# Attention in chunks of 64 tokens instead of 128, with 64 by 64 products, a scan for the states and a new order of the engines

## The chip, the cores and the metric

The kernel runs on one core of a Trainium2 chip. A core has TensorE (matrix products, PE in the profile; its weight loads are listed as PEld), VectorE (DVE), ScalarE (ACT), GpSimd (POOL) and SyncE (SP, which issues the DMAs here). The metric is the device time of one execution in microseconds (us); the median of three executions counts.

## The reference, cut to what matters

Three stages follow each other on inputs of 2 batches, 768 tokens and 8 heads of 48 channels. The change lies in the first.

```python
def _attn_ref(r, k, v, w, u):              # each (2, 8, 768, 48); u is (8, 48)
    state = np.zeros((B, H, D, D))
    for t in range(S):
        kt, vt, rt, wt = k[:, :, t], v[:, :, t], r[:, :, t], w[:, :, t]
        cur = np.einsum('bhd,bhe->bhde', u[None] * kt, vt)
        y[:, :, t] = np.einsum('bhd,bhde->bhe', rt, state + cur)
        state = wt[:, :, :, None] * state + np.einsum('bhd,bhe->bhde', kt, vt)
```

The second stage, on the heads joined to 384 channels, is a gated layer: `h = gelu(x @ w_in)`, its half `v` is normalised, mixed over the tokens by `w_sg`, multiplied with the half `u`, sent through `w_out` and added to `x`. The third stage mixes each token with the one before it and computes `sigmoid(xr @ w_r) * (relu(xk @ w_k)**2 @ w_v)`.

## The kernel before, in words

The tokens of a batch are cut into two halves of 384 (`TB`); batch and half give the group g = 0 to 3. A unit of attention is one group and one pair of heads, so there are 16 units (`units`, 4 in each group). The two heads of a pair lie on partitions 0 to 47 and 64 to 111. The sequential recurrence is replaced by chunks of `C` = 128 tokens. Within a chunk the running products of the decays w are made by a scan of VectorE, r is multiplied and k is divided by them, and what remains are matrix products. The preparation is done for packs (12, three in each group; the fourth pair of a group is collected from spare partitions of the three packs by DMAs into the tile `six`).

The steps, with the letter that each has in the written order: for a pack, `L` and `q` load, `D` (L267) and `g` (L274) are the two scans of 387 elements, `j` (L271) takes reciprocals, `d` (L278) multiplies r and k in, `K` (L282) makes r times k, `f` is a check on ScalarE, `6` moves the spare rows. For a unit, `w` loads v; `T` (L327) transposes the keys on TensorE and `k` (L331) copies them out of PSUM on ScalarE; `A` (L338) are the scores of keys against queries, `P` (L345) the sums for the present token; `m` (L378) masks the scores and `n` (L384) weighs v, both on VectorE out of PSUM; `S` (L354) are the products keys times v of one chunk; `s` (L365) adds the state before to them by a product with the identity, and `x` (L373) multiplies with the chunk's decay on ScalarE, which gives the state after the chunk; `J` (L394), `N` (L398) and `I` (L404) add up the output in PSUM; `O` (L408, L411) copies it out on ScalarE and `o` shares the fourth pair's rows out by DMAs.

The other letters are dense stages on full 128 by 128 products: `v` and `u` are the two halves of `x @ w_in`, `M` the mixing over tokens, `W` the product with `w_out`, `E`, `R` and `Z` the products of the third stage. `C` converts weights (`x`, `b`, `t` and `o` are VectorE's parts of it, `h` is ScalarE's; C0 to C2 are the weights that `v` needs, C3 to C5 those of `u`), `X` splits x into a high and a low part, `e` is a product whose result nobody reads and which keeps TensorE busy. `v0.2` is the first dense product; it needs the splits X0.2 and the weights C0, C1 and C2. A generator token such as `v0.2` stands once for each of its steps.

All instructions are issued in the order of one string, `ORDER` (L37): a token emits its instructions, each engine executes its own in that order, and semaphores are placed by the framework from the tiles that are read and written. The fp32 products of the attention stand in the trace as two loads and two matmuls each; the dense ones are three products of rounded halves (`mm3`, L207 to L209).

PSUM has eight banks here: three for `ps_d` (dense products), two for the scores `pA` (`ps_A`), two buffers of one bank for the outputs `py` (`ps_y`), one for `ptr` and `pkv` (`ps_t`).

Of the kernel before, what the change touches and what calls it, by code (L numbers as in the profile page):

```python
# [36 lines left out]
ORDER = """L0 D0 j0 e e e e e e e g0 f0 e L1 D1 q0 d0 j1 e e e e e e e e K0 g1 Q q1 L2 w0 q2 w1 A0 P0 T0 e e e e e e f1 k0 S0.0 S0.1 x0.0 m0 d1 n0 K1 J0 s0.1  # L37
S0.2 A1 x0.1 s0.2 P1 x0.2 C1.l D2 j2 g2 m1 d2 C1.x n1 61 w2 L3 K2 C1.b C0.l 60 62 e T1 e e N0 k1 S1.0 S1.1 x1.0 J1 s1.1 S1.2 I0 A2 x1.1 s1.2 P2 C1.r
x1.2 f2 O0 e e T2 e D3 n2 m2 j3 C0.x C0.b C0.t C1.t g3 e N1 k2 S2.0 S2.1 x2.0 J2 s2.1 S2.2 I1 A3 C1.q O1 P3 x2.1 s2.2 x2.2 f3 w3 q3 L4 m3 K3 D4 n3 j4
d3 e e T3 N2 e e k3 S3.0 S3.1 C0.h x3.0 J3 s3.1 S3.2 N3 x3.1 I3 O3 A4 I2 s3.2 P4 x3.2 e T4 e e e k4 w4 q4 C2.l C2.r S4.0 s4.0 S4.1 L5 x4.0 g4 d4 K4 n4  # L40
m4 A5 s4.1 P5 J4 C5.l o3 w5 q5 o3 D5 C0.o C2.x m5 n5 j5 f4 O2 x4.1 C1.h 63 o3 T5 k5 N4 e e S5.0 s5.0 S5.1 J5 x5.0 C2.q s5.1 x5.1 X0.2.h X0.0.h N5 I4
I5 C2.b g5 d5 K5 C2.t T6 C2.h C5.r k6 w6 64 L6 w7 X0.2.l C1.o C2.o v0.2 S6.0 s6.0 S6.1 65 X0.0.l D6 C5.x j6 C5.b A7 C5.q X0.1.h x6.0 O4 C0.r s6.1 g6
O5 f6 x6.1 P7 C5.t C5.h v0.0 T7 n7 m7 v0.2 k7 A6 S7.0 P6 s7.0 S7.1 J7 X0.1.l q6 C3.l C3.x K6 C3.b n6 d6 C5.o C7.l C4.l C4.x w8 L7 q7 q8 m6 C3.t C4.b
C4.t C0.q x7.0 s7.1 C7.h C3.r x7.1 v0.1 N7 T8 I7 A8 v0.0 f5 k8 C3.h O7 C3.q C4.h v0.0 C3.o D7 P8 S8.0 S8.1 J6 N6 o7 j7 C4.o n8 g7 m8 d7 u0.0 u0.3 I6
A9 C4.r x8.0 v0.0 f7 s8.1 S8.2 C7.o K7 P9 m9 O6 v0.1 x8.1 J8 s8.2 v0.0 x8.2 u0.0 C8.l C9.l w10 o7 L8 C11.l L9 w9 o7 D8 K8 j8 g8 d8 n9 q9 B 68 66 N8
u0.1 T9 u0.2 v0.1 v0.2 k9 C9.h S9.0 S9.1 C8.h X1.0.h X1.2.h x9.0 u0.2 C11.h C11.o X1.0.l C9.o X1.2.l I8 A10 P10 s9.1 S9.2 x9.1 J9 s9.2 v0.2 x9.2
X1.1.h X1.1.l u0.1 v0.1 v1.0 N9 T10 C8.o 67 D9 j9 n10 m10 v0.0 C4.q f8 k10 u0.3 u1.1 S10.0 S10.1 I9 A11 x10.0 O8 P11 s10.1 S10.2 x10.1 v1.0 J10 q10
w11 C6.l C16.l L10 s10.2 u1.2 x10.2 C6.h v0.2 T11 v1.0 v1.1 C10.l K9 g9 d9 D10 j10 K10 n11 v0.2 C6.o g10 m11 O9 u1.2 v0.1 f9 v0.1 v1.0 k11 C10.h C10.o
v1.2 S11.0 S11.1 J11 v1.1 x11.0 s11.1 S11.2 x11.1 v1.2 d10 A12 s11.2 P12 C19.l w12 C14.l L11 x11.2 v1.1 u1.0 N10 T12 u1.1 C14.h C14.o m12 n12 N11 u1.3
I11 v1.2 k12 v1.1 C16.h C16.o v1.2 O11 u1.0 A13 I10 O10 S12.0 P13 s12.0 S12.1 J12 x12.0 v1.0 v1.0 s12.1 C15.l C15.h x12.1 v1.1 w13 C17.l o11 q11 v1.2  # L50
o11 69 o11 X2.0.h C19.r v1.1 v1.2 D11 j11 g11 d11 m13 n13 K11 C15.o N12 M0.1 T13 M0.2 M0.2 A14 I12 X2.2.h X2.1.h X2.1.l C19.x C19.b C19.t C17.h C17.o
k13 P14 S13.0 f11 s13.0 S13.1 J13 611 C13.l w14 w15 C12.l 610 C24.l m14 n14 M0.1 x13.0 s13.1 x13.1 O12 u1.3 f10 C19.q M0.0 N13 T14 I13 C13.h k14 A15
P15 m15 X2.0.l M0.2 M0.1 C13.o S14.0 s14.0 S14.1 J14 x14.0 s14.1 C24.r x14.1 C12.h O13 N14 v2.0 T15 n15 M0.0 X2.2.l C24.x C24.b C24.t M0.3 M0.3 C18.l
k15 S15.0 s15.0 S15.1 J15 x15.0 s15.1 x15.1 N15 I15 O15 C24.q C12.o I14 O14 C21.l | C19.h C24.h C21.r v2.2 v2.2 C21.q v2.0 C18.r C18.q C19.o C24.o
C21.x v2.1 M0.0 C18.x M0.3 C18.b C18.t C21.b C21.t M1.1 C26.l C20.l v2.2 C18.h C18.o M1.1 M1.2 C26.r v2.2 C26.x M1.1 M1.2 M1.3 M1.0 v2.1 G0.3.h C21.h
C21.o v2.1 v2.0 C20.x C26.b C20.b C20.t C26.t M1.3 M1.3 C26.h v2.1 v2.0 v2.0 v2.2 v2.1 u2.2 v2.0 C20.h G0.3.l M1.0 M1.0 v2.1 u2.0 G0.1.h G0.0.h G0.0.l
G0.1.l v2.2 C20.o u2.2 C26.q u2.1 u2.3 u2.0 u2.1 G0.2.h u2.3 C20.r o15 o15 o15 X3.2.h C20.q C34.l C27.l C27.r X3.1.h C25.l C27.q C25.r X3.0.h C25.q
C27.x G0.2.l W0.2 W0.0 C27.b C27.t X3.1.l C26.o W0.2 v3.1 W0.1 X3.0.l X3.2.l v3.1 C25.x W0.1 C25.b v3.1 v3.2 v3.0 C27.h C27.o C25.t v3.1 v3.1 C34.x
C34.b W0.0 v3.2 v3.0 v3.0 v3.2 u3.3 u3.2 u3.3 u3.0 u3.1 u3.2 v3.0 C34.r C25.h C25.o C34.t v3.0 C23.l C22.l C28.l v3.2 C34.q u3.1 v3.2 v3.1 v3.0 C22.r
G1.3.h G1.0.h G1.1.h v3.2 M2.3 M3.2 C22.x M1.2 C22.b C22.t C22.h u3.0 C22.q C34.h C22.o M3.2 M3.2 C34.o C28.x C28.b C28.t C28.h C28.o G1.0.l M2.1 M2.1  # L60
C28.r C28.q G1.2.h C35.l C35.x M2.2 M2.2 C23.x C37.l M3.3 C35.r C35.b C35.t G1.2.l C35.h C35.q C35.o G1.3.l C38.l C23.b C23.t C23.h C38.r M2.2 M2.3
G1.1.l M2.3 M2.0 C23.o M2.0 M2.0 M3.3 W1.0 W1.0 C37.x W1.2 W1.1 C38.x M2.1 G2.1.h G2.1.l C38.b G2.0.h G2.0.l W1.1 C37.b W1.2 C38.q C37.r C37.q G2.2.h
G2.2.l M3.0 M3.1 G2.3.h G2.3.l C37.t C23.r M3.0 H0 Y0.0.0.a C38.t Y0.0.2.a Y0.1.0.a M3.3 C31.l C29.l C36.l W2.2 M3.1 Y0.0.1.a C23.q Y0.1.0.b C31.r
Y0.0.0.b Y0.0.1.b Y0.0.0.c W2.2 Y0.0.1.c C37.h C37.o Y0.1.2.a C31.q Y0.0.2.b Y0.0.2.c M3.0 M3.1 C36.x W2.0 W2.1 W2.1 Y0.1.1.a C36.b C36.t E0.0 C36.r
Y0.1.2.b C36.q E0.0 C36.h Y0.1.1.b E0.0 Y0.1.0.c C36.o W2.0 E0.2 E0.0 C38.h E0.1 E0.5 Y0.1.1.c Y0.1.2.c C38.o E0.0 C31.x E0.1 F E0.2 C31.b C31.t C29.x
R0.0 R0.0 C29.r E0.1 E0.1 G3.0.h R0.2 E0.2 C29.b C29.t E0.1 C29.h C29.o C30.l C32.l C33.l E0.3 E0.4 G3.1.h E0.3 E0.2 C31.h E0.3 C31.o R0.2 E0.3 E0.3
E0.5 C32.x C30.x C30.b C30.t G3.3.h C30.h E0.5 G3.3.l C30.o E0.2 E0.7 R0.1 R0.1 E0.6 C29.q C33.x C33.b C33.t E0.4 E0.4 C32.b C32.t C32.h C33.h E0.4
C33.o E0.5 E0.5 C32.o E0.4 E0.6 E0.6 E0.7 E0.7 E0.7 E0.6 H1 E0.6 C33.r Y1.0.0.a Y1.0.0.b Y1.0.2.a E0.7 C33.q Y1.0.1.a Y1.1.1.a Y1.0.0.c Z0.0 Z0.1 Z0.2
Z0.3 Z0.4 Z0.5 Z0.6 Z0.7 Y1.0.1.b Y1.0.2.b Y1.0.1.c Y1.0.2.c E1.0 E1.0 E1.0 Y1.1.0.a Y1.1.0.b E1.0 E1.0 z0.1 E1.2 E1.2 E1.1 E1.5 z0.2 E1.2 E1.1 E1.1
E1.1 E1.2 Y1.1.2.a Y1.1.2.b Y1.1.2.c E1.2 E1.5 Y1.1.1.b G3.1.l E1.5 E1.5 E1.1 E1.6 E1.6 Y1.1.0.c z0.0 E1.5 E1.3 Z1.0 Z1.1 E1.4 E1.7 Z1.2 E1.3 E1.3  # L70
E1.3 G3.2.h G3.0.l E1.3 Z1.3 E1.6 Y1.1.1.c E1.6 E1.6 G3.2.l R1.0 W3.2 y0.1 y0.2 y0.0 H2 Y2.0.0.a Y2.0.1.a Y2.0.0.b Y2.0.1.b E1.4 E1.4 E1.4 Y2.0.1.c
Y2.0.2.a Y2.0.0.c Y2.0.2.b Y2.0.2.c E2.0 E2.0 Y2.1.1.a E1.4 R1.1 Z1.4 Z1.5 Z1.6 R1.0 R1.1 E1.7 E1.7 Y2.1.0.a W3.2 E1.7 E1.7 Z1.7 R1.2 W3.0 E2.1 E2.0
# [851 lines left out]
```

## Time and profile before

| | us |
|---|---|
| median of 3 runs | 332.86 (332.62 to 333.13) |
| the profiled execution | 332.0 |
| its span, first to last instruction | 330.2 |
| first dense product starts (in the span) | 36.66 |
| last product of the attention, next dense product starts | 116.76 |
| TensorE busy | 321.7 |
| VectorE busy | 232.7 |

Times in rows are microseconds from the span's start unless marked ns. A row of instructions gives the engine, the line of the code, the operation, what it writes and reads, the shape and how many there were (x12). Matmuls are pipelined and their listed durations overlap: what one costs is read from the distance between starts.

### The profile page before, as it was taken

How to read it: one execution, taken by the hardware profiler on the slowest of the kernel's cores; microseconds unless marked ns; L12 is line 12 of the kernel's file. 1: busy time of each engine (PE TensorE's matmuls, PEld its weight loads, DVE VectorE, ACT ScalarE, POOL GpSimd, SP SyncE). 2: the span in 40 equal slices, each digit the busy share in tenths (PEclk: the TensorE clock that was granted, in tenths of full speed). 3: DMA queues.
4: the chain of work that ended last, by engine and by line, in shares of the span. 5: the costliest groups of instructions: out<-in, count | busy, mean ns of one | idle time of the engine just before them, and what ended most of it. 6: DMA issues, size and time to landing. Idle time of an engine off the chain costs nothing.

```text
span 330.2 us, 6938 instructions
## 1 busy us (share of the span) xinstructions
PE 321.7 (97%) x2721; PEld 299.3 (91%) x2721; DVE 232.7 (70%) x427; ACT 180.9 (55%) x440; POOL 28.6 (9%) x78
## 2 busy tenths in 40 slices
...
GB/s 188 229 272 208 141 217 177 209 196 113 77 84 178 98 70 109 64 128 66 48 95 50 4 143 48 95 3 0 48 26 0 3 48 21 5 0 24 50 24 54
DMA packets 16501, 29.82 MB, mean 90 GB/s; under 512 B 2256, under 2 KB 12496, under 8 KB 16464
## 3 DMA queue, kind: packets, MB, share of 16 engines
...
q8 instruction: 22, 0.36, 0.4%
q14 instruction: 15, 0.12, 0.1%
...
## 4 chain that ended last, share of the span: by engine, by line
PE 91%; DVE 3%; DMA 2%; ACT 1%; POOL 1%; issue 1%; SPq 0%; ACTq 0%; DVEq 0%
PE po L565 12%; PE pk L207 5%; PE ps L207 5%; PE pk L208 5%; PE pk L209 5%; PE ps L209 5%; PE ps L208 5%; PE po L209 4%; PE po L208 4%; PE po L207 4%; PE pA L338 3%; PE pu L207 3%; PE py L394 3%; PE py L404 3%; PE pu L209 3%; PE pu L208 3%
## 5 line engine op out<-in xcount | busy, mean ns | idle before, releaser
L539 DVE TENSOR_TENSOR kr<-kr 128x384 f32<-128x384 f32 x32 | 17.4, 555 | 22.5 <-ACT kr L537 22.3
L207 PE MATMUL ps<-wsg,vn_hi 128*128 128x384 f32 x96 | 32.8, 341 | 0.0
L207 PE MATMUL pk<-xk_hi,wk_hi 128*128 128x384 f32 x96 | 32.6, 339 | 0.0
L209 PE MATMUL pk<-xk_hi,wk_lo 128*128 128x384 f32 x96 | 32.5, 338 | 0.0
L208 PE MATMUL pk<-xk_lo,wk_hi 128*128 128x384 f32 x96 | 32.5, 338 | 0.0
L209 PE MATMUL ps<-wsg,vn_lo 128*128 128x384 f32 x96 | 32.4, 338 | 0.0
L208 PE MATMUL ps<-wsg,vn_hi 128*128 128x384 f32 x96 | 32.4, 338 | 0.0
L537 ACT ACTIVATE kr<-pk 128x384 f32<-128x384 f32 x32 | 15.6, 491 | 24.9 <-PE pk L209 18.8
L544 ACT CAST kk_hi<-kr 128x384 fp32r<-128x384 f32 x32 | 16.0, 511 | 19.1 <-DVE kr L539 14.9
L546 DVE TENSOR_TENSOR kk_lo<-kr,kk_hi 128x384 fp32r<-128x384 f32 x32 | 17.7, 555 | 11.7 <-ACT kk_hi L544 11.2
L565 PE MATMUL po<-pl_win_hi,kk_hi 128*128 128x384 f32 x81 | 23.1, 339 | 0.0
L565 PE MATMUL po<-pl_win_lo,kk_hi 128*128 128x384 f32 x63 | 18.4, 339 | 0.0
L207 PEld LDWEIGHTS pk<-xk_hi,wk_hi 128*128 128x128 f32 x96 | 18.0, 188 | 0.3 <-DVE xT L504 0.3
L565 PE MATMUL po<-pl_win_hi,kk_lo 128*128 128x384 f32 x54 | 18.3, 339 | 0.0
L207 PE MATMUL pu<-xs_hi,win_hi 128*128 128x384 f32 x48 | 16.9, 352 | 1.4 <-ACT v L453 1.4
L207 PEld LDWEIGHTS ps<-wsg,vn_hi 128*128 128x128 f32 x96 | 18.0, 188 | 0.1
L208 PEld LDWEIGHTS ps<-wsg,vn_hi 128*128 128x128 f32 x96 | 18.0, 188 | 0.0
L208 PEld LDWEIGHTS pk<-xk_lo,wk_hi 128*128 128x128 f32 x96 | 18.0, 188 | 0.0
L209 PEld LDWEIGHTS ps<-wsg,vn_lo 128*128 128x128 f32 x96 | 18.0, 188 | 0.0
L209 PEld LDWEIGHTS pk<-xk_hi,wk_lo 128*128 128x128 f32 x96 | 18.0, 188 | 0.0
L378 DVE TENSOR_TENSOR am<-pA,c_sb 128x768 f32<-128x768 f32 x16 | 15.1, 946 | 3.3 <-PE pA L345 3.3
L208 PE MATMUL po<-ga_lo,wout_hi 128*128 128x384 f32 x48 | 16.2, 337 | 0.0
(208 smaller groups left out, 902.2 us busy)
## 6 DMA issues: line engine op xcount, KB each, us to landing
...
```

Source lines behind the costliest of these rows:

```text
L207: T.matmul(ps, lh, rh, start=(i == 0), stop=False)
L208: T.matmul(ps, lh, rl, start=False, stop=False)
L209: T.matmul(ps, ll, rh, start=False, stop=(i == n - 1))
L338: T.matmul(u.pA[q:q + 64, h, c * C:(c + 1) * C], u.kinv[o:o + D, c, q:q + 64], u.rp[o:o + D, c, :], start=True, stop=True)
L378: V.tensor_mul(u.am.rearrange("p h (c t) -> p h c t", c=NCB), u.pA[:, :, :TB].rearrange("p h (c t) -> p h c t", c=NCB), mask[:, None, None ...
L394: T.matmul(u.py[64 * h:64 * h + m, cs], u.vk[:, c, h * D:h * D + m], u.am[:, h, cs], start=(c == 0), stop=False)
L404: T.matmul(u.py[o:o + D, c * C:(c + 1) * C], u.state(c)[o:o + D, :], u.rp[o:o + D, c, :], start=False, stop=(c == NCB - 1))
L537: A.activation(kr, ps, AF.Relu)
L539: V.tensor_mul(kr, kr, kr)
L544: A.copy(hi, kr)
L546: V.tensor_sub(lo, kr, hi.bitcast(F32))
L565: T.matmul(pv[g][s], l, wv[i][r], start=st, stop=(i == KF - 1 and l is ll))
```

## The change: what it does

Chunks have 64 tokens (`CA`), six in a half (`NA`). Each product of the attention is cut so that its operands are at most 64 by 64, and the four pairs of (rows 0 or 64, columns 0 or 64) of the array are taken in turn (`QUAD`). This holds for `A`, `P`, `S`, `J` and `N`; `I` has its rows and columns on the same head, so it uses two of the four. `N` is now an ordinary product with the identity instead of a transposition. `s` is gone. `x` happens once in a unit instead of once in a chunk: ScalarE copies all six products of keys and v out of PSUM, for the second half VectorE adds the state that the first half left, and one scan of VectorE over 48 times 7 elements makes all states (each row of seven ends with a zero, which restarts it). The decays that it multiplies with are laid out by a second copy of ScalarE in `k`. The scans of a pack write a tile `sc` of which there is one, `d` writes the packed tile, `j` also copies the chunk decays on GpSimd. `pA` and `pkv` now share one pair of banks (`tag="ab"`, one buffer), and `py` is one buffer of two banks. The four multiplications that made `uu` on GpSimd are gone. The order of all engines is new; it has 44 `e` instead of 39.

```diff
+CA = 64
+NA = TB // CA
-WL = NCB * (C + 1)
-PK = 2 * WL + TB
+WL = NA * (CA + 1)
+PK = 3 * TB + NA
-    ps_y = ctx_a.enter_context(tc.tile_pool(name="ps_y", bufs=2, space=PSUM))
+    ps_y = ctx_a.enter_context(tc.tile_pool(name="ps_y", bufs=1, space=PSUM))
+    QUAD = ((0, 0), (1, 1), (0, 1), (1, 0))
         def decays(u):
+            u.sc = ap1.tile([P, 2 * WL + 2], F32, name=f"sc_{u.n}", tag="sc")
+            V.tensor_tensor_scan(u.sc[:, :WL], u.wt[:, :WL], d1pat, 0.0, ALU.mult, ALU.add)
         def divide(u):
+            u.pk = ap3.tile([P, PK], F32, name=f"pk_{u.n}", tag="pk")
+            d = d1w.rearrange("p (c j) -> p c j", c=NA)[:, :, CA:CA + 1]
+            V.reciprocal(d, chunks(u.sc, 0)[:, :, CA:CA + 1])
+            G.tensor_copy(u.pk[:, 3 * TB:], chunks(u.sc, 0)[:, :, CA:CA + 1].rearrange("p c o -> p (c o)"))
         def keys(u):
             A.copy(u.kT, u.ptr)
+            u.fd, u.kv = fds[u.i % 2], kvs[u.i % 2]
+            A.copy(u.fd[:, :, :NA], u.W[:, None, :].broadcast_to([R, D, NA]))
         def scores(u):
+            u.pA = ps_A.tile([P, 2, 512], F32, name=f"pA_{u.n}", tag="ab")
             for c in range(NCB):
-                for h, q in ((0, 0), (1, 64), (0, 64), (1, 0)):
-                    o = 64 * h
-                    T.matmul(u.pA[q:q + 64, h, c * C:(c + 1) * C], u.kinv[o:o + D, c, q:q + 64], u.rp[o:o + D, c, :], start=True, stop=True)
+                for h, q in QUAD:
+                    o, t, s0 = 64 * h, 64 * q, c * C + q * CA
+                    T.matmul(u.pA[t:t + 64, h, c * CA:(c + 1) * CA], u.kinv[o:o + D, s0:s0 + CA], u.rp[o:o + D, s0:s0 + CA], start=True, stop=True)
         def sums(u):
...
+                for h, q in QUAD:
+                    o, t = 64 * h, 64 * q
+                    k = u.home()[o:o + D, 2 * TB + c * C + t:2 * TB + c * C + t + CA]
+                    T.matmul(u.pA[t:t + 64, h, NCB * CA + c:NCB * CA + c + 1], k, c_sb[o:o + D, CU + u.p:CU + u.p + 1], start=True, stop=True)
         def states(u, c):
...
+                u.pkv = ps_A.tile([P, 2, 512], F32, name=f"pkv_{u.n}", tag="ab")
+                u.sx = ap2.tile([R, D, NA + 1], F32, name=f"sx_{u.n}", tag="sx")
+            for h, q in QUAD:
+                o, t, m = 64 * h, 64 * q, (64, D)[h]
+                T.matmul(u.pkv[o:o + m, q, c * D:(c + 1) * D], u.kT[t:t + 64, c, o:o + m], u.vk[t:t + 64, c, h * D:(h + 1) * D], start=True, stop=True)
-        def carry(u, c):
-            for h in range(2):
-                o, m = 64 * h, (64, D)[h]
-                T.matmul(u.pkv[o:o + m, c, :], ident[:, o:o + m], u.state(c), start=False, stop=True)
         def fade(u, c):
-            A.activation(o, u.pkv[:R, c, :], AF.Copy, scale=u.W[:, c, :])
+            A.copy(u.kv[:, :, :NA].rearrange("r e (c q) -> r e c q", q=2), u.pkv[:R, :, :NCB * D].rearrange("r q (c e) -> r e c q", c=NCB))
+            if u.hf:
+                V.tensor_add(u.kv[:, :, 0], u.kv[:, :, 0], Slast[u.p])
+            flat = "r e n -> r (e n)"
+            V.tensor_tensor_scan(u.sx.rearrange(flat), u.kv.rearrange(flat), u.fd.rearrange(flat), 0.0, ALU.add, ALU.mult)
+            if not u.hf:
+                Slast[u.p] = ap1.tile([R, D], F32, name=f"sl_{u.n}", tag=f"sl{u.p}")
+                G.tensor_copy(Slast[u.p], u.sx[:, :, NA - 1])
         def weigh(u):
-            u.am = ap2.tile([P, 2, TB], F32, name=f"am_{u.n}", tag="am")
+            u.am = ap2.tile([P, 2, NCB * CA], F32, name=f"am_{u.n}", tag="am")
...
         def inner(u):
...
+                for h, q in QUAD:
+                    o, t, m = 64 * h, 64 * q, (64, D)[h]
+                    T.matmul(u.py[o:o + m, q, c * CA:(c + 1) * CA], u.vk[t:t + 64, c, h * D:h * D + m], u.am[t:t + 64, h, c * CA:(c + 1) * CA], start=(c == 0), stop=False)
         def inject(u):
             for c in range(NCB):
-                T.matmul(u.py[:, c * C:(c + 1) * C], u.vg[:, c, :R], eye, start=False, stop=False, is_transpose=True)
+                for h, q in QUAD:
+                    o, t, m = 64 * h, 64 * q, (64, D)[h]
+                    T.matmul(u.py[o:o + m, q, c * CA:(c + 1) * CA], u.vg[t:t + 64, c, o:o + m], eye[t:t + 64, t:t + 64], start=False, stop=False)
         def outer(u):
...
+                for h, q in QUAD:
+                    n, o = 2 * c + q, 64 * h
+                    if u.state(n) is not None:
+                        T.matmul(u.py[o:o + D, q, c * CA:(c + 1) * CA], u.state(n)[o:o + D, :], u.rp[o:o + D, n * CA:(n + 1) * CA], start=False, stop=(c == NCB - 1))
```

Of the order, the stretch from unit 5's states to the first dense product and on to unit 8's, before and after:

```text
before: ... S5.0 s5.0 S5.1 J5 x5.0 C2.q s5.1 x5.1 X0.2.h X0.0.h N5 I4 I5 C2.b g5 d5 K5 C2.t T6 C2.h C5.r k6 w6 64 L6 w7
X0.2.l C1.o C2.o v0.2 S6.0 s6.0 S6.1 65 X0.0.l D6 C5.x j6 C5.b A7 C5.q X0.1.h x6.0 O4 C0.r s6.1 g6 ...
after:  ... j5 m5 n5 g5 C1.o d5 C1.q C2.h k5 O4 S5.0 J5 N5 S5.1 S5.2 e x5.0 K5 T6 A6 I5 P6 o3 o3 o3 C3.l w6 63 64 w7 65
X0.1.h X0.2.h C2.r X0.0.h C2.q O5 f5 k6 X0.2.l C3.x C2.o C4.x v0.2 n6 m6 C3.b X0.1.l S6.0 S6.1 J6 N6 S6.2 X0.0.l C3.t C4.b
L6 x6.0 D6 T7 v0.1 A7 P7 I6 C4.r v0.2 ... m7 C5.x n7 C5.b C5.t j6 w8 q6 C5.h v0.0 S7.0 S7.1 J7 N7 S7.2 C4.o C5.o u0.0 u0.3
... x7.0 ... A8 P8 I7 D7 m8 n8 ... T8 O7 k8 C5.r v0.2 u0.3 J8 N8 S8.0 S8.1 S8.2 ...
```

## Rows read from the trace of the kernel before

**Rows 1.** The page: span and busy time of the engines.

```profile
span 330.2 us, 6938 instructions
PE 321.7 (97%) x2721; PEld 299.3 (91%) x2721; DVE 232.7 (70%) x427; ACT 180.9 (55%) x440; POOL 28.6 (9%) x78
```

**Rows 2.** Windows by stage: length, busy time of each engine (instructions), clock, DMA.

```profile
3.43:38.30 34.87, 34.40 (x536) 25.06 (x535) 34.22 (x56) 17.70 (x49) 5.34 (x11) 1.00 0.73 217
36.66:58.60 21.94, 21.44 (x305) 17.65 (x305) 19.98 (x34) 17.05 (x46) 1.25 (x3) 1.00 0.66 198
58.60:116.76 58.16, 58.16 (x728) 52.69 (x724) 40.68 (x69) 37.92 (x99) 7.81 (x21) 1.00 0.48 136
```

**Rows 3.** Timeline of VectorE and then TensorE at the first dense product.

```profile
36.60 0.56 DVE L441 TENSOR_TENSOR xs_lo<-xT,xs_hi 128x384 fp32r<-128x384 f32 x1
37.08 1.29 DVE L175 TENSOR_TENSOR win_lo<-winv_x,win_hi 128x512 fp32r<-128x512 f32 x2
...
38.62 0.40 PE L208 MATMUL pv<-win_lo,xs_hi 128*128 128x512 f32 x1
38.86 0.40 PE L209 MATMUL pv<-win_hi,xs_lo 128*128 128x512 f32 x1
39.18 0.32 PE L354 MATMUL pkv<-vk,kT 128*64 128x48 f32 x4
```

**Rows 4.** VectorE's groups from the start to 38.3 us.

```profile
L267 DVE TENSOR_TENSOR_SCAN pk<-wt,d1pat 128x387 f32<-128x387 f32 x6 | 5.7, 953 | 2.5 <-DMA wt<-in_wp_dram 2.5
...
L378 DVE TENSOR_TENSOR am<-pA,c_sb 128x768 f32<-128x768 f32 x6 | 5.7, 943 | 0.0
L282 DVE TENSOR_TENSOR pk<-rk 128x384 f32<-128x384 f32 x6 | 3.3, 546 | 0.0
...
L154 DVE TENSOR_SCALAR winv_x<-winv_raw 128x512 int32<-128x512 int32 x3 | 1.3, 425 | 0.3 <-DMA winv_raw<-in_w_in_dram 0.2
...
L271 DVE RECIPROCAL d1w<-pk 128x3 f32<-128x3 f32 x6 | 1.0, 170 | 0.1
```

**Rows 5.** Timeline of TensorE, units 14, 12 and 13 between two dense products.

```profile
97.28 0.89 PE L338 MATMUL pA<-pk 48*64 48x128 f32 x24
97.99 0.39 PE L404 MATMUL py<-pk,sl 48*48 48x128 f32 x4
...
98.74 0.52 PE L345 MATMUL pA<-uu,pk 112*64 112x2 f32 x12
99.11 0.29 PE L354 MATMUL pkv<-vk,kT 128*64 128x48 f32 x4
...
99.40 0.28 PE L394 MATMUL py<-am,vk 128*48 128x128 f32 x1
...
100.06 0.35 PE L365 MATMUL pkv<-sx,c_sb 112*48 112x48 f32 x4
...
103.57 0.49 PE L398 MATMUL py<-c_sb,vg 128*112 128x128 f32 x3
103.89 0.45 PE L327 MATMUL ptr<-c_sb,pk 112*128 112x112 f32 x3
```

**Rows 6.** Timeline, first scores: matmuls begun by 7.48 us, loads begun by 7.60 us.

```profile
7.45 0.34 PE L338 MATMUL pA<-pk 48*64 48x128 f32 x4 [0.27 <-DVE pk L278]
...
7.45 0.21 PEld L338 LDWEIGHTS pA<-pk 48*64 48x64 f32 x8 [0.76 <-DVE pk L278]
```

**Rows 7.** ScalarE's groups by form.

```profile
L373 ACT ACTIVATE sx<-pkv,pk 112x48 f32<-112x48 f32 x24 | 7.2, 299 | 9.9 <-PE pkv L354 9.3 <-PE pkv L365 0.5
...
L331 ACT COPY kT<-ptr 128x336 f32<-128x336 f32 x16 | 6.9, 433 | 6.3 <-PE ptr L327 6.3
```

**Rows 8.** Timeline of SyncE: issue of the constants; the page's line on their DMA (KB, us to landing).

```profile
2.50 0.58 SPq L646 DMA_DIRECT2D c_sb<-in_cst_dram  x1
...
c_sb<-in_cst_dram SPq DMA_DIRECT2D x1, 191.0 KB, 4.4
```

**Rows 9.** Timeline of TensorE, the longest wait behind the attention.

```profile
154.04 0.45 PE L207 MATMUL pu<-xs_hi,win_hi 128*128 128x384 f32 x1 [1.43 <-ACT v L453]
```

More of the change, by code (lines that the diff above doesn't have):

```diff
@@ L53 @@
[L53 to L56, printed above, removed]
@@ L86 @@
 WCH = 384
-CM, CI, CB, CU, CG, CMK, CMR = 0, 128, 256, 368, 372, 376, 379
-NCONST = 382
+CM, CI, CB, CU, CG, CMK, CMR, CH = 0, 128, 256, 368, 372, 376, 379, 382
+NCONST = 446
 @with_exitstack
@@ L103, in fused_kernel @@
     c_sb = keep.tile([P, NCONST], F32, name="c_sb")
-    mask = c_sb[:, CM:CM + C]
+    mask = c_sb[:, CH:CH + CA]
     ident = c_sb[:R, CI:CI + R]
@@ L221, in fused_kernel @@
     over = keep.tile([P, B * NB * KX], F32, name="over")
-    Wall = keep.tile([P, B * NB * KX * NCB], F32, name="Wall")
+    Wall = keep.tile([P, B * NB * KX * NA], F32, name="Wall")
     G.memset(Wall, 0.0)
```

156 lines of the change are left out of this document (70 added, 86 removed).

## The prediction

> **What bounds the kernel now.** I read the page first: TensorE is busy in 97% of the span [rows 1]. Then the windows, cut where the kind of work changes, because the bound is not the same throughout. Up to 38.3 us VectorE works 34.22 of 34.87 us: it is the bound, and TensorE's high share there holds products `e` that nobody reads. From 36.66 us, where `v0.2` begins, to 116.76 us, where the last attention product is out, TensorE is busy in all but half a microsecond of 80.1 us and at full clock, VectorE in 60.7 [rows 2]. Behind that TensorE runs dense products alone, which the change doesn't touch. So two terms count: how much later or earlier `v0.2` can start, which VectorE decides, and how much TensorE work lies behind its start. What sets the first: the split `xs_lo` starts at 36.60, the last two weight parts run to 38.37, and `v0.2` finishes just behind, its last product at 38.86 [rows 3].
>
> **TensorE, one round.** A round is one load and one matmul on each of the four tiles; an fp32 product counts as two matmuls, so `A`, `P`, `S`, `J` and `N` of a unit are 24 matmuls, six rounds, each. Today's scores already use four tiles with 128 moving columns: 24 matmuls from 97.28 to 97.99, 0.71 us. The sums use two tiles with two columns: 12 matmuls from 98.74 to 99.11, 0.37 us, which is 62 ns for each pair, and cannot be streaming; it is the load of 64 columns [rows 5]. Can four tiles load at once? At the first scores, which begin at 7.45 us, four matmuls have begun by 7.48 us and eight loads by 7.60 us [rows 6]: the second load on every tile is under way within 0.15 us of the first. So I take the sums' 60 ns for a round of four tiles, 0.36 us for six. I take 55 ns as the lower bound (the same row less what it takes to get going) and, as the upper one, the best sustained rate that a row shows: `S` and `s`, 12 matmuls from 99.11 to 99.40, 24 ns each [rows 5], 97 ns for a round.
>
> **TensorE, the sum behind the start of `v0.2`.** In the old order units 6 to 15 have all but one `T` behind it; in the new order `A6`, `P6` and `T6` are in front, where VectorE is the bound.
> - `A`: 10 of 0.71 before, 9 of 0.36 after: -3.9 us. `P`: 10 of 0.37, 9 of 0.36: -0.5.
> - `S` with `s`: 44 groups of four matmuls at 0.10 (three from 99.11 to 99.40), against 30 groups of two rounds, 0.12: -0.7.
> - `J`: 99.40 to 100.06, 0.66, against 0.36, ten times: -3.0. `N`: 103.57 to 103.89, 0.32, against 0.36: +0.4.
> - `I` stays on two tiles. Twelve matmuls took 97.99 to 98.74 less the change of tile shape below, 0.66; a pair of loads and matmuls with 64 columns goes at the sums' rate, 0.72 for 24 and 0.60 for 20 (eight took two thirds of 0.66 before). Six of the ten units lie in the second half of a batch (twelve and 24), four in the first: +1.0.
> - A change of tile shape drains the array: dense products start 0.24 us apart, but `S` of another shape 0.32 behind one [rows 3]; 0.08, and I take 0.09. Counted along the written orders, 38 such changes before and 41 after: +0.3.
>
> Together -6.4 us. With 97 ns for a round the 288 rounds of four tiles (48 groups of six: nine each of `A` and `P`, ten each of `S`, `J` and `N`) cost 10.7 us more, and the sum is +4.3.
>
> A rule speaks against this change. The Trainium skill, "TensorEngine Tiling (Array Packing)", section "Instruction Overhead", says that each matmul costs some 60 cycles, so that one of a single column takes as long as one of 60, and that no tiling should be taken from a dimension that is small already. If it held for matmuls on different tiles, a round would be about 100 ns (an estimate from its figure at 2.4 GHz), and the sum about +5. The trace disagrees as far as it goes: on four tiles four matmuls begin within 40 ns [rows 6].
>
> **VectorE in front of `v0.2`.** Instructions overlap: 0.56 us long, but 0.48 to the next start [rows 3], so I take 0.08 off each listed duration. Added: a scan of 336 elements for each of units 0 to 5. The row is 953 ns for 387 [rows 4]; scaled, 0.83, a slot of 0.75, six times 4.5 us (bounds: unscaled, 5.2; at the rate of the 384-element product, 546 ns [rows 4], 2.4). Two additions of 48 elements: between the reciprocal's 170 ns of three elements and that scaled from 384 elements, 0.12 each after overlap, 0.2. Removed: half of six masks, 943 ns for 768 elements, 546 ns for 384 [rows 4], -0.40 each, -2.4. Moved in front of the last weight part: `C3.x`, 425 ns [rows 4], 0.34. Reciprocals of six elements instead of three: nothing, they are all overhead. Sum: +2.7 us (0.6 to 3.4). VectorE is busy 98% there, so nothing hides this: `v0.2` finishes at about 41.9 instead of 39.2 [rows 3].
>
> **What I cost at nothing.** Behind `v0.2` VectorE gains ten scans and six additions and loses half of ten masks, +4.2 us on 60.7 in a stretch of now some 76: 85%, hidden under TensorE; without that cover it costs up to 4.2. ScalarE: a second copy in `k` and one copy in `x` (288 elements each, under the 433 ns of 336) for 40 activations of 299 ns [rows 7]: 12.6 against 12.0 us in all, and it is busy 55 of 80 us. GpSimd's copies, on an engine busy 9% [rows 1], have a ScalarE copy as their first reader. On SyncE the constants are issued one load later, behind the second `rk` [rows 8]: landing about 8.1 instead of 6.9; VectorE's first mask is at its place at about 9.2, so it isn't late. The four more `e` ahead of `A0` run while these constants are under way.
>
> **New waits.** `pA` and `pkv` share one buffer: `S` of a unit stands behind its `m` and `n` on VectorE, and the next `A` behind ScalarE's copy. Queued behind `S` on TensorE is everything. In the new order a dense product of 1.6 to 3.2 us stands between `P` and the first of `S` for eight of the nine units from 7 on, against 0.84 us of `m` and `n`; for unit 8 only `I7` and `T8`, and about half a microsecond shows. Today's attention stretch has waits of that kind too (I assume as many again), and there is one of 1.4 us ahead of 154.04 [rows 9] that the new order may keep or lose.
>
> **Sum.** The profiled execution took 332.0 us, 1.8 more than its span: 332.0 - 6.4 + 2.7 = 328.3. The median of the runs is 0.9 above that execution, so 329.2 us.
>
> **Rivals.**
> 1. Rounds are fed too slowly. At 97 ns the time is 329.2 + 10.7 = 339.9. For it: no row shows more than one matmul in 24 ns over a dozen. Against it: the burst of the first scores, and that those dozen were bound by their loads. Break-even with before is at 72 ns. By the page quoted above this rival is what happens.
> 2. VectorE holds the products in the attention stretch: every unit from 7 on waits for `n` before `S`. From 36.66 to 58.60 VectorE is busy 19.98 of 21.94 us [rows 2], it starts 2.7 us late and has more to do there. From the point where each of nine units waits 0.4 us the gain is gone; at 0.6 the time is 334.6. Against it: from 58.60 on VectorE works 40.7 of 58.2 us.
> 3. The late start is made up: the 1.4 us of [rows 9] go, and as much again of the waits in the attention stretch, which the old order also has. Then 329.2 less 3.0 us: 326.2.
> 4. Little happens: rounds at some 70 ns, or half of rival 2: 332.2 to 333.5.
>
> **How the numbers follow.** My forecast, 327.3 to 331.6 about 329.2, has 0.42; rival 3 0.15; rival 4 0.09; rival 2 0.20; rival 1 0.14. A difference of 0.2% (0.7 us) is what measuring can tell: faster 0.57, same 0.09, slower 0.34. The range reaches from rival 3's lower part to beyond rival 2's price and leaves most of rival 1 out: 325.8 to 337.0. It holds cases of both signs; the likeliest alone is 327.3 to 331.6.
>
> **What would show it.** Right: six rounds of scores take 0.33 to 0.40 us between starts; `v0.2` ends 2 to 3.5 us later; the dense product behind `I15` starts earlier by 1.5 to 5, allowing for one more `v` in front of it. Wrong: rounds of 80 ns or more; TensorE idle ahead of `S` with VectorE's `n` named; a scan of 336 elements far from 0.83 us; or a longer wait around the second batch's `v` and `u`.

## The result, and the profile after

| | before | after |
|---|---|---|
| median of 4 executions each, on one chip | 332.74 us | 336.6 us |
| ratio, with its 95% interval | | 1.0121 [1.0096, 1.0145] |
| the profiled execution, its span | 332.0, 330.2 us | 336.34, 334.4 us |
| first dense product `v0.2` starts | 36.66 us | 45.61 us |
| from there to TensorE's last product | 289.7 us | 285.0 us |

The change made the kernel slower by 1.2%; I had forecast 329.2 us. Ratios, here and below, leave out executions over 1.5% longer than the fastest one of the same kernel; medians and ranges are of all executions. The last two lines of the table say where the time went: the stage in front of `v0.2` became 8.95 us longer (I had 2.7), the stage behind it 4.7 us shorter (I had 6.4).

The page after: span, busy times, and from its second part the clock that TensorE was granted, in 40 slices (they answer to [rows 1]).

```profile
span 334.4 us, 8994 instructions
PE 319.8 (96%) x3734; PEld 296.3 (89%) x3734; DVE 239.5 (72%) x451; ACT 182.3 (54%) x432; POOL 44.3 (13%) x98
...
PEclk9996999999999999999999999999999999999998
```

The fourth slice is new: before, the clock was whole in every slice. The windows show the stages (for [rows 2]): up to `v0.2` before (first line) and after, the stretch of the lower clock, and from `v0.2` to 128.40, which is one step of `v` behind the last product of the attention.

```profile
3.43:36.66 33.23, 32.76 (x531) 24.06 (x529) 32.58 (x53) 16.06 (x46) 5.34 (x11) 1.00 0.73 220
...
3.43:45.61 42.18, 36.27 (x957) 26.21 (x955) 36.22 (x62) 19.16 (x49) 8.18 (x24) 0.92 0.63 193
...
28.30:35.10 6.80, 6.80 (x143) 4.95 (x135) 5.00 (x10) 2.37 (x6) 1.62 (x3) 0.50 0.78 243
45.61:128.40 82.79, 80.14 (x1632) 70.02 (x1629) 65.09 (x118) 56.50 (x143) 21.84 (x37) 1.00 0.52 144
```

In the row up to 45.61 us VectorE works 36.22 of 42.18 us and stands still for 5.96. Before, from 3.43 to 36.66 us, it worked 32.58 of 33.23 and stood still for 0.65. So of the 8.95 us, 3.6 are more work and 5.3 are waiting: VectorE no longer bounds this stage alone. Who it waits for, from 8 to 50 us (us in total, times, longest):

```profile
DVE sx L377 <- ACT kv L373: 3.9, 2, 2.1
DVE winu_x L156 <- DMA winu_raw<-in_w_in_dram: 1.3, 1, 1.3
DVE winv_x L156 <- DMA winv_raw<-in_w_in_dram: 0.6, 1, 0.6
DVE kv L375 <- ACT kv L373: 0.3, 1, 0.3
```

Two scans of states, of units 2 and 3, wait 2.13 and 1.80 us for ScalarE's copy, and this copy waits for `S` on TensorE. (The wait of 1.3 us lies behind the start of `v0.2`, at 46.35 us; it delays the last weight part, for which `v0.2` then waits 0.4 us.) TensorE's timeline shows why `S2` is late:

```profile
23.74 0.57 PE L400 MATMUL py<-am,vk 64*64 64x64 f32 x24
24.12 0.54 PE L406 MATMUL py<-c_sb,vg 64*48 64x64 f32 x24
24.49 0.20 PE L363 MATMUL pkv<-vk,kT 64*64 64x48 f32 x1
26.81 0.56 PE L363 MATMUL pkv<-vk,kT 64*64 64x48 f32 x23 [2.12 <-issue]
27.87 0.63 PE L346 MATMUL pA<-pk 48*64 48x64 f32 x24 [0.51 <-ACT kv L373]
```

One matmul of `S2.0` runs, the other 23 follow 2.3 us later, and no semaphore is named: "issue" is time in which the engine waited for nothing that the profile shows. The transfers point to it. TensorE's own instructions are loaded in packets of 16 KB (queue q8); the page counts 30 of them after and 22 before, one for some 250 recorded TensorE instructions (matmuls and loads together, 7468 and 5442). The transfer view of 18.7 to 24.5 us has data only, that of 24.5 to 25.6 us has one such packet:

```profile
DMA packets 583, 1.36 MB, mean 235 GB/s; under 512 B 82, under 2 KB 338, under 8 KB 583
...
q8 instruction: 1, 0.02, 5.4%
```

It ran from 24.60 to 25.55, behind 1.36 MB of loads; when it was asked for, the trace doesn't show. After this standstill the granted clock fell to 0.50, 1.2 instead of 2.4 GHz, from 28.3 to 35.1 us (the row of this stretch above), and `J3`, `N3` and `S3` took nearly twice their time.

What stands right in front of `v0.2` is TensorE's own queue. These lines are from the timelines of VectorE and TensorE:

```profile
43.27 0.86 DVE L377 TENSOR_TENSOR_SCAN sx<-kv,fd 112x336 f32<-112x336 f32 x1
44.18 0.39 PE L413 MATMUL py<-pk,sx 48*48 48x64 f32 x4 [0.36 <-DVE sx L377]
44.49 0.55 DVE L451 TENSOR_TENSOR xs_lo<-xT,xs_hi 128x384 fp32r<-128x384 f32 x1
45.14 0.54 PE L354 MATMUL pA<-c_sb,pk 48*64 48x1 f32 x20
45.61 0.50 PE L209 MATMUL pv<-win_hi,xs_hi 128*128 128x512 f32 x1
```

`I5` waits for the scan of unit 5's states, and `I5` and `P6` follow it until 45.61 us. VectorE's split `xs_lo` is done at 45.04; it is not what `v0.2` starts on.

Of the rounds, a timeline of `T`, `A` and `P` of unit 9 and `I` of unit 8 answers to [rows 5]:

```profile
66.64 0.45 PE L333 MATMUL ptr<-c_sb,pk 112*128 112x112 f32 x3
67.02 0.58 PE L346 MATMUL pA<-pk 48*64 48x64 f32 x24
67.42 0.48 PE L354 MATMUL pA<-c_sb,pk 48*64 48x1 f32 x24
67.75 1.08 PE L413 MATMUL py<-pk,sx 48*48 48x64 f32 x20
68.75 0.45 PE L209 MATMUL pu<-xs_hi,win_hi 128*128 128x384 f32 x1
```

`A` takes 0.40 us to the next start and `P` 0.33, near the 0.36 forecast; `I` with 20 matmuls takes 1.00 (0.83 from its first to its last), where I had 0.60. Its weight loads, grouped by form from 45 to 130 us (busy, mean ns):

```profile
L413 PEld LDWEIGHTS py<-pk,sx 48*48 48x48 f32 x145 | 7.5, 178 | 0.0
L413 PEld LDWEIGHTS py<-pk,sl 48*48 48x48 f32 x16 | 1.4, 125 | 0.1
```

A load of 48 columns from `sl`, where they are neighbours, takes 125 ns; from `sx`, where the scan leaves them every 28 bytes, 178.

The dense product behind `I15`, the last of the attention, started at 116.76 us before and starts here:

```profile
126.26 0.50 PE L209 MATMUL pv<-win_hi,xs_hi 128*128 128x512 f32 x1
```

From the start of `v0.2` to there are 80.10 us before and 80.65 after, with one step of `v` more in it (2.2 us, 126.26 to 128.44). So the stretch of the attention became some 1.6 us shorter, and 3.1 of the 4.7 us came from behind it, where the change touches no product: 1.4 of them are the wait of [rows 9], which is gone.

VectorE's groups up to 48 us answer to [rows 4]: the scan and the mask have the sizes that I used.

```profile
L377 DVE TENSOR_TENSOR_SCAN sx<-kv,fd 112x336 f32<-112x336 f32 x6 | 5.1, 851 | 4.1 <-ACT kv L373 3.9
L385 DVE TENSOR_TENSOR am<-pA,c_sb 128x384 f32<-128x384 f32 x6 | 3.2, 530 | 0.0
...
L375 DVE TENSOR_TENSOR kv<-kv,sl 112x48 f32<-112x48 f32 x2 | 0.5, 246 | 0.3 <-ACT kv L373 0.3
```

### The profile page after: what moved, and what is told of

Read it like the earlier page. It is cut to its first block, busy times and chain, and to the rows that moved or that the text cites. A ratio compares the mean times of both kernels' runs of the same rounds, so it can differ in the third digit from the quotient of the medians.

```text
span 334.4 us, 8994 instructions
## 1 busy us (share of the span) xinstructions
PE 319.8 (96%) x3734; PEld 296.3 (89%) x3734; DVE 239.5 (72%) x451; ACT 182.3 (54%) x432; POOL 44.3 (13%) x98
## 4 chain that ended last, share of the span: by engine, by line
PE 78%; DMA 4%; DVE 2%; ACT 2%; SPq 2%; issue 1%; DVEq 0%; ACTq 0%
PE po L575 11%; PE pk L210 5%; PE pk L209 5%; PE pk L211 5%; PE ps L209 5%; PE ps L211 5%; PE ps L210 5%; PE po L211 4%; PE po L210 4%; PE po L209 4%; PE pu L209 2%; PE py L413 2%; PE pu L211 2%; PE pu L210 2%; PE pv L209 2%; PE pr L211 2%
## 5 line engine op out<-in xcount | busy, mean ns | idle before, releaser
L377 DVE TENSOR_TENSOR_SCAN sx<-kv,fd 112x336 f32<-112x336 f32 x16 | 13.7, 855 | 7.8 <-ACT kv L373 7.3
L211 PE MATMUL po<-ga_hi,wout_lo 128*128 128x384 f32 x48 | 16.2, 337 | 0.0
```

Source lines behind the costliest of these rows:

```text
L211: T.matmul(ps, ll, rh, start=False, stop=(i == n - 1))
L377: V.tensor_tensor_scan(u.sx.rearrange(flat), u.kv.rearrange(flat), u.fd.rearrange(flat), 0.0, ALU.add, ALU.mult)
```

## The experiments

Theory 1: `v0.2` is late because TensorE's instructions come late and because its clock falls behind such standstills; behind `v0.2` the outer products cost more for the step at which they read the states. Theory 2: the order of the products makes the first stage late, wherever packets and clock fall. Each ratio is against the kernel before on the same chip.

**One load later.** The 512 KB load of `C2` goes behind the next `w`.

```diff
-S2.0 S2.1 S2.2 C2.l w4 C1.b
+S2.0 S2.1 S2.2 w4 C2.l C1.b
```

> Only the load of one 512 KB weight part (C2.l, issued at 20.64 us on SyncE) goes behind the load of unit 4's vk, which SyncE issued at 27.4. Theory 1, TensorE's late instructions: in the changed kernel 23 of the 24 matmuls of S2.0 waited from 24.49 to 26.81 us for an instruction block whose packet (24.60 us) stood behind a burst of loads; VectorE's scans x2.0 and x3.0 waited 2.13 and 1.80 us for what came of it, and the granted clock fell to half. Then without this load in the burst S2.0 takes some 0.1 us, those two waits shrink to under 0.5 us each, v0.2 starts 2.5 to 4.5 us earlier than 45.6, and the time is 332 to 334 against 336.6. Theory 2, the order of the products itself makes the first stretch late: the gap at S2.0 goes or moves, but v0.2 still starts at 44.5 to 46 and the time stays at 335.8 to 337. Against both: C2's words land some 0.5 to 1 us after VectorE's first use of them.

Measured: 335.31 us, ratio 1.0118 [1.0077, 1.0158]. The packet came at 23.74 instead of 24.60 us, the gap became shorter and did not go:

```profile
24.52 0.20 PE L363 MATMUL pkv<-vk,kT 64*64 64x48 f32 x1
26.03 0.56 PE L363 MATMUL pkv<-vk,kT 64*64 64x48 f32 x23 [1.31 <-issue]
```

The lower clock came later and lasted 3.4 us (39.9 to 43.3) instead of 6.8, and `v0.2` started at 44.80, 0.8 us earlier: in theory 2's range, not in theory 1's. The ratio is that of the kernel after. So loads ahead of the packet delay it, but moving 512 KB took away less than half of the gap.

**States read from neighbouring places.** The outer products read 48 neighbouring elements of the scan's buffer, which are not the states.

```diff
-            return u.sx[:, :, c - 1]
+            return u.sx.rearrange("r e n -> r (e n)")[:, (c - 1) * D:c * D]
```

> The outer products load the states as 48 neighbouring elements of the same buffer instead of every seventh (28 bytes apart); the instructions and their number are unchanged, the values loaded are not the states, so the output is not the reference's. Theory 1, the load's step: weight loads of I from sx fall from 179 ns to about 125, as those from sl; 24 matmuls of I take 0.66 to 0.72 us instead of 0.94 and 20 take 0.55 to 0.60 instead of 0.83; ten of them stand behind the start of v0.2, so the time falls by 1.5 to 2.6 us, to 334 to 335.1. Theory 2, a load with a matmul of 64 columns does not fit into 60 ns on two tiles: I stays at 0.83 to 0.94 us and the time at 336 to 337.

Measured: 334.16 us, ratio 1.0057 [1.0031, 1.0082]. The loads, from 45 to 130 us:

```profile
L413 PEld LDWEIGHTS py<-pk,sx 48*48 48x48 f32 x144 | 5.0, 120 | 0.0
```

24 matmuls of `I` took 0.64 us from first to last start instead of 0.94, 20 took 0.53 instead of 0.83. The step of the load is the cause of the slow `I`; that a load with a matmul of 64 columns doesn't fit into a pair's 60 ns is refuted. `v0.2` started at 45.53, as late as in the kernel after.

**Both together.**

> Both edits of the two runs before together (output not the reference's, as there: the outer products load other values than the states). If late instructions and the step of the state's loads are two separate causes, the gains add: 329.5 to 332. If the first stretch is late for its order alone, 333.5 to 335.

Measured: 334.82 us, ratio 1.0086 [1.0049, 1.0124], with executions from 332.3 to 336.4. The spread is as wide as the gains, and goes with the clock: mean 0.995 in the fastest, 0.977 in the slowest. The gains did not add: the time is in the second of the two ranges.

**The full computation with copied states**, and the load moved. The scan's buffer `sx` is single here.

```diff
-                u.sx = ap2.tile([R, D, NA + 1], F32, name=f"sx_{u.n}", tag="sx")
+                u.sx = ap1.tile([R, D, NA + 1], F32, name=f"sx_{u.n}", tag="sx")
...
-                G.tensor_copy(Slast[u.p], u.sx[:, :, NA - 1])
+            G.tensor_copy(u.sc.rearrange("r n e -> r e n"), u.sx[:, :, :NA])
```

> The full computation: GpSimd copies the scan's six states into one contiguous buffer (288 elements, in place of its copy of the last state, 48 elements), the outer products load from there; and the 512 KB load moved as in the first run. If GpSimd's copy (estimate 0.6 to 1.0 us from its other copies) stays hidden: within 0.7 us of the run with both edits, 329.5 to 332.5, so at or below the kernel before (332.7). Rival: GpSimd's queue, where the next pack's copy stands behind this one, or the one sx buffer, makes scans and outer products wait: 333.5 to 336.

Measured: 340.1 us, ratio 1.0274 [1.0213, 1.0335], longer than both ranges. GpSimd's copy takes 1064 ns, and `I` waits for it, nine times, 8.7 us in all (waits of TensorE's loads):

```profile
PEld py L414 <- POOL sl L379: 8.7, 9, 1.5
```

**Instruction blocks shifted.** Fourteen `e` at the start are cut into four each; nothing else moves.

```diff
-f0 e e e e e e e e e e e e e e e e q1
+f0 e e i i i i i i i i i i i i i i q1
```

> Fourteen of the 16 products e ahead of q1 are each cut into four with 128 columns: the same columns, but 84 more TensorE instructions before 7.3 us, and nothing else. TensorE's instructions come in packets of 16 KB, one for about 252 recorded instructions; the one that S2.0 waited for was asked for behind some 694 and needed at 946. Theory 1 (late instructions): the packet is now asked for 84 instructions earlier, ahead of the burst of loads issued from 19.05 us on; S2.0 runs in about 0.1 us without its gap of 1.5 to 2.3 us, v0.2 starts 2 to 4.5 us before 45.6, and the time is 332.5 to 335 against 336.6, though there is more to execute. Theory 2 (the order of the products makes the first stretch late, wherever the packets fall): v0.2 starts at 44.5 to 46.5 and the time is 336 to 338.

Measured: 334.93 us, ratio 1.0074 [1.0048, 1.0101]. The same packet, the third, came at 18.67 us and `S2.0` ran in one piece. `v0.2` started at 45.17 all the same, in theory 2's range, while the time is in theory 1's: the clock was at half in three stretches of 3.4 us (from 23.1, 29.9 and 40.1 us), the first after waits of 0.6 and 0.8 us ahead of `S1.0` and `A3`. So taking the gap away is not enough, and the clock also falls without it.

**More fill.** Fourteen more `e` in TensorE's waits (the expectation says sixteen; the order has fourteen).

```diff
-J1 N1 e e k1
+J1 N1 e e e e k1
...
-x1.0 e T2 A3
+x1.0 e e e T2 A3
```

> Sixteen more products e (0.22 us each) where TensorE stood still in the first stretch: 2 behind N1, 2 behind x1.0, 2 behind S2.2, 4 behind T4, 2 behind S4.1, 2 behind S5.0 and so on, placed in waits of 0.6 to 1.6 us. Theory 1a: the granted clock, which fell to half for 6.8 us (about 28.8 to 35.6), falls because TensorE stood still; then more of the stretch is at full clock (mean 0.990 or more instead of 0.986) and the time falls by 1 to 2 us, though the gap at S2.0 stays. Theory 2: the added products only delay what stands behind them on TensorE: 336.5 to 339.

Measured: 338.09 us, ratio 1.0141 [1.0092, 1.0189], theory 2's range. `v0.2` started at 47.31, and the clock was at half for 6.8 us as before, from 28.9. The timeline shows the gap again:

```profile
24.54 0.53 PE L406 MATMUL py<-c_sb,vg 64*48 64x64 f32 x21
27.49 0.27 PE L406 MATMUL py<-c_sb,vg 64*64 64x64 f32 x2 [2.43 <-issue]
```

The gap is now in `N2`, eight instructions earlier in the order: four more `e` of a load and a matmul each stand ahead of it. Counted from the start, it lies behind TensorE's 948th recorded instruction, here as in the kernel after and in the first three runs. It belongs to a place in the instruction stream and not to a product.

**Fewer instructions.** `P` and `N` go back to the two-tile and the transposed form, 60 TensorE instructions less for a unit. The edit of `N`:

```diff
-                for h, q in QUAD:
-                    o, t, m = 64 * h, 64 * q, (64, D)[h]
-                    T.matmul(u.py[o:o + m, q, c * CA:(c + 1) * CA], u.vg[t:t + 64, c, o:o + m], eye[t:t + 64, t:t + 64], start=False, stop=False)
+                for q in range(2):
+                    t = 64 * q
+                    T.matmul(u.py[:R, q, c * CA:(c + 1) * CA], u.vg[t:t + 64, c, :R], eye[t:t + 64, t:t + 64], start=False, stop=False, is_transpose=True)
```

> P and N as they were before, fitted to the new places: P on two tiles with two columns (12 matmuls instead of 24), N as six transposes (6 matmuls instead of 24). TensorE has 60 instructions less for each unit, 960 of some 7500. Theory 1 (late instructions): S2.0 has no gap, the granted clock stays above 0.993, v0.2 starts 2.5 to 5 us earlier than 45.6, and behind it P and N cost about what they did (P +0.05, N -0.05 to +0.1 us a unit): 332 to 334. Theory 2 (order): v0.2 at 45 to 46, time 336 to 337.5.

Measured: 337.57 us, ratio 1.0161 [1.0093, 1.0229]. No gap, and `v0.2` starts at 43.57, 2.0 us earlier: less than theory 1's 2.5 to 5, but earlier than theory 2's 45 to 46. But the clock is at half from 44.1 to 47.5, and each `P` and `N` now stands between two changes of tile shape (0.15 us from the last start to the next, where it was 0.04). The stage behind `v0.2` is 1.8 us longer than in the kernel after, and the time lies at the upper end of theory 2's range.

**ScalarE copies the states.**

```diff
+        def line(u):
+            A.copy(u.sc.rearrange("r n e -> r e n"), u.sx[:, :, :NA - 1])
```

> The full computation: ahead of each I ScalarE copies the five states that I takes from the scan (240 elements) into neighbouring places, and I loads them from there. By the run with states read flat (334.2) the load's step costs 2.4 us; ScalarE gets 16 copies of about 0.35 us, 10 of them behind the start of v0.2, where it is busy about 55 to 60%. If they are hidden: 334 to 335.2. If they delay kT, kv or the dense products' activations in ScalarE's queue by 0.2 us or more a unit: 336 to 338.

Measured: 342.8 us, ratio 1.0243 [1.0182, 1.0305]. The copy of 240 elements takes 621 ns, where the copy of 288 out of PSUM takes 402:

```profile
L384 ACT COPY sc<-sx 112x240 f32<-112x240 f32 x15 | 9.3, 621 | 12.5 <-DVE sx L377 11.2 <-DVE d1w L276 1.3
L373 ACT COPY kv<-pkv 112x288 f32<-112x288 f32 x16 | 6.4, 402 | 18.0 <-PE pkv L363 18.0
```

It holds up ScalarE's queue, and `I` waits for it (6.4 us in nine waits of TensorE's loads). I had 336 to 338 for this case; `v0.2` started at 51.03, after three stretches of half clock.

**No fill**, and with it a buffer of its own for `pkv`, both on the kernel with fewer instructions. The first edit stands for all twelve `e` between `P2` and `v0.2` (the expectation says 19; the order has twelve), the second holds for units 0 to 5:

```diff
-J1 N1 e e k1
+J1 N1 k1
...
-                u.pkv = ps_A.tile([P, 2, 512], F32, name=f"pkv_{u.n}", tag="ab")
+                u.whole = pkv = ps_A.tile([P, 2, 512], F32, name=f"pkv_{u.n}", tag="ab") if u.i > 5 else None
+                u.pkv = [pkv[:, q, :] if u.i > 5 else ps_d.tile([P, 512], F32, name=f"pkv{q}_{u.n}", tag="d") for q in range(2)]
```

> The run with fewer instructions (P and N as before the change; v0.2 at 43.57 us there, no gap at S2.0), with the 19 products e between P2 and v0.2 left out as well: nobody reads them. Theory 3: what is left of the late start is a chain in which TensorE, ScalarE and VectorE wait for each other, because pA and pkv share one buffer and py has only one; e stands in that chain with 0.2 to 0.4 us each wherever S, A or J doesn't wait anyway: v0.2 starts 0.5 to 2 us earlier, 41.5 to 43. Theory 4: VectorE's own work sets the start; v0.2 stays at 43 to 44. The granted clock may fall earlier for want of e: then J, N and S take twice their time for 3.4 or 6.8 us, and v0.2 comes later than 44.

> The same, and in units 0 to 5 pkv gets two banks of its own (from those of the dense products, free at that time), copied by two ScalarE activations instead of one. S then no longer waits for m and n of the next unit on VectorE, nor A for ScalarE's copy of pkv. Theory 3 (the shared buffer): the 0.7 us ahead of A3, A4 and A5 go, VectorE's waits for pA and kv shrink, and v0.2 starts 1 to 2.5 us earlier than in the run before this one. Theory 4 (VectorE's own work): within 0.5 us of it.

Measured: 342.07 us, ratio 1.0291 [1.0237, 1.0346], and 342.5 us, 1.0304 [1.024, 1.0369]. Without `e` the clock was at half for 30.7 us, 23.9 to 54.7, and `v0.2` started at 49.19 instead of 43.57. Page of the first of the two:

```profile
span 340.3 us, 8012 instructions
...
PEclk9995557999999999999999999999999999999998
```

Leaving `e` out costs more here than it saves; whether the chain would be shorter at the full clock is not shown. With its own banks for `pkv`, `v0.2` is at 49.44: under this clock the shared buffer is not what counts, and at full clock it wasn't tried.

**All edits of order together.** Shifted blocks, the later load, and 14 `e` in TensorE's waits; two of the places:

```diff
-S2.0 S2.1 S2.2 C2.l w4 C1.b D4 x2.0 A4
+S2.0 S2.1 S2.2 w4 C2.l C1.b D4 x2.0 e e A4
...
-S5.0 J5
+S5.0 e e J5
```

> The full computation with three edits of order only: the shifted instruction blocks (84 instructions more before 7.3 us), the 512 KB load behind unit 4's vk, and 14 more products e in the waits of the first stretch (2 ahead of S1.0, 3 ahead of A3, 2 ahead of A4, 2 behind T4, 2 ahead of J4, 2 ahead of J5, 1 ahead of I5). If the late instruction packet and the clock that falls behind it and behind the other waits are what made the first stretch late beyond VectorE's own 2.7 us: no gap above 1 us at S2.0, clock 0.995 or more in most runs, v0.2 starts at 41.5 to 43.5, time 332 to 333.5. If the fill stands in the way of the chain, or packets are late elsewhere: v0.2 at 44.5 or later, 334.5 to 337.

Measured: 333.43 us, ratio 1.0027 [0.9997, 1.0057]: by the ratios 3.1 us less than the kernel after, and not to be told from the kernel before. No gap at `S2.0`, the clock whole, `v0.2` at 43.71, just behind the range that I gave:

```profile
3.43:43.71 40.28, 36.55 (x1002) 28.22 (x1007) 36.62 (x63) 18.70 (x49) 8.34 (x24) 1.00 0.68 204
```

VectorE still stands still for 3.66 us, now for loads (0.9, 0.8 and 0.3) and ScalarE's copies (0.7 and 0.4). So at `v0.2` the three edits took away 1.9 of the 8.95 us; 7.05 are left, 4.0 of work and 3.0 of waiting. Of the twelve executions, eight had a mean clock of 0.997 or more; seven of these took 331.0 to 333.5 us, one 335.7. The four at 0.987 to 0.995 took 335.7 to 338.2.

**The same with states read flat.**

> The same with the outer products loading neighbouring elements of the scan's buffer (values other than the states, so the output is not the reference's). If the causes add: 1.5 to 2.6 us less than the run before this one, 329.8 to 331.8, near the 329.2 predicted for a first stretch bound by VectorE alone and outer products at 60 ns a pair. If not: what is gained behind v0.2 is lost in other waits, and it stays within 0.7 us of the run before this one.

Measured: 333.9 us, ratio 1.0019 [0.999, 1.0048]. The forecast sum fails here: nothing is gained on the run before. In its trace the third packet is late again (22.20 us; TensorE stands still for 0.80 us in `J2`, behind its 946th recorded instruction), the clock is at half for 3.4 us, `v0.2` starts at 44.61, and behind it TensorE waits 1.2 us for `kT`, 0.9 for a DMA and 0.8 for ScalarE's `uT`. From `v0.2` to the last product it takes 284.0 us, against 284.1 in the run before. What the shorter `I` is worth in the end lies between nothing (here) and some 2 us (the first run with it).

## Why the prediction was wrong, point by point

**The step that failed** is the one that costs VectorE in front of `v0.2`: "VectorE is busy 98% there, so nothing hides this: `v0.2` finishes at about 41.9". The work was sized well (scan 851 ns against 0.83 forecast, masks 530 against 546; the two additions took 0.34 each to the next start where I had 0.12; 3.6 us more work up to `v0.2`, of which some 1.1 are the split `xs_lo` and one weight part, which stood beside and behind its start before). What failed is the premise that VectorE stays the bound and is never kept waiting. I took [rows 2] as a property of the stage; it held for the old TensorE stream, which was still for 0.47 us only (3.43 to 36.66 us). After the change it has 957 matmuls up to `v0.2` instead of 531, shorter ones, and pauses between them. Its instruction packet came late, its clock fell, and VectorE, which needs `S` through ScalarE for its new scan, waited 5.3 us more. `v0.2` finished at about 48.2. The same premise put TensorE's own work there at nothing ("`A6`, `P6` and `T6` are in front, where VectorE is the bound"). In the kernel after, `I5` and `P6` alone stand for 1.5 us between VectorE's scan of unit 5's states and `v0.2`; in the run with all edits `T6`, `A6`, an `e`, `I5` and `P6` follow each other for 3.0 us, from 40.71 to 43.71, with VectorE's split done at 43.14.

How far this is shown: the packet's place by six kernels with the gap behind the same 948th instruction (the kernel after, the first three runs, more fill, ScalarE's copies) and by two in which an earlier packet (18.67 and 19.00 us) left no gap. TensorE went on 1.3 to 1.4 us behind the packet's end whenever it had waited for it (25.55 to 26.81; 24.67 to 26.03 with the later load; 23.17 to 24.49 in the last run). That a long stretch of half clock costs several us is shown by the run without fill, +5.6 us at `v0.2` against the same kernel with fill. What its 6.8 us cost in the kernel after was not measured alone, and that the gap brought it down is argued from the order in time only: with a gap of 1.3 us the clock stayed whole for another 13 us, and with shifted blocks and with fewer instructions it fell without the gap. The three edits together account for 3.1 us of the time and 1.9 us at `v0.2`. The larger part of the late start stays open: VectorE's waiting in the run with all edits, 3 us more than before, and TensorE's queue in front of `v0.2` were not taken apart.

The 336.6 us lie within the range that I gave, 325.8 to 337.0, but by luck: its upper part stood for rival 2, which is not what happened.

**The second step** is a term of the sum: "`I` ... a pair of loads and matmuls with 64 columns goes at the sums' rate, 0.72 for 24 and 0.60 for 20". They took 0.94 and 0.83 from first to last start, since each load from `sx` takes 178 ns instead of 120 to 125; read flat they took 0.64 and 0.53. The layout stood in the diff (`u.sx[:, :, c - 1]`), and I priced the load by the shape alone. The Trainium skill has the rule: "SBUF — State Buffer", section "Door 1: The DMA port swizzle (why `[64,N]` ≈ `[32,N]`)", says that consecutive accesses run at full bandwidth only within a line of 16 bytes, four fp32 values. The 28 bytes here cross a line with every element, and the trace agrees, 178 against 120 in the run with flat reads.

The other terms, from the distances between starts from `v0.2` on, before and after (waits included): `A` -5.4 us (forecast -3.9), `J` -2.8 (-3.0), `S` with `s` -2.6 (-0.7), `P` -0.5 (-0.5), `N` +0.2 (+0.4), `I` +4.9 (+1.0), `v` +1.1, `T` +0.9 and `M` +0.5 (the shape changes, +0.3, and waits), `W` and `Z` -0.9. Sum -4.7 against -6.4. The products of the attention alone, `A` to `I`, came to -6.1, near the forecast of -6.7, because `A` and `S` made up for `I`. What stands under `v`, `T` and `M`, waits of 2.3 us among it (`S6`, `S10`, `J14`), took most of that back.

**A round of four tiles: right.** 24 matmuls in 0.36 us between first and last start, 60 ns a round as forecast. Rival 1 is refuted, and with it, for products on different tiles, the rule on 60 cycles for each matmul that I weighed ("TensorEngine Tiling (Array Packing)" of the Trainium skill, section "Instruction Overhead"): its 100 ns for a round (an estimate from its figure) would be 25 ns a matmul; measured are 15.

**Rival 2**, VectorE holding `S` behind `v0.2`: one wait of 0.8 us (`S6`, for the mask), none of note behind; not what happened. **Rival 3:** the 1.4 us of [rows 9] did go, and no wait took their place there. So half of this rival came true; without it the stage behind `v0.2` would be 3.3 us shorter instead of 4.7. **Costed at nothing:** right for GpSimd's small copies and the constants' DMA (`P0` waits 0.6 us for it, VectorE doesn't); ScalarE was not always hidden, as the next waits show. **New waits:** `J` waits for ScalarE's copy out of `py`'s only buffer, twice some half a microsecond ahead of `v0.2`, and `S10` 1.1 us for ScalarE's `kT`. The half microsecond that I had for unit 8 did not show, and beyond unit 8 I had none.
